# Two attention steps back to back in a fused attention and MLP kernel, the second one in the MLP's activation banks

## The chip, the cores and the metric

The kernel runs on one core of a Trainium2 chip. The metric is the device time of one execution in microseconds; the kernel before takes 1001.8 us (median of three runs, 1000.68 to 1001.87). The core has five engines that run side by side: TensorE (PE in the profile) for matmuls, VectorE (DVE), ScalarE (ACT), GpSimd (POOL), and SyncE (SP), which issues the transfers here. Matmul results go to PSUM, a small memory of eight banks, 512 float32 columns by 128 partitions each.

## The reference

A kernelised (random feature) attention feeds an MLP with layer normalisation and a residual. Batch 8, 8 heads, sequence 576, head dimension 64, 128 features; the model width is 512 and the hidden width 2048, and the sequence rows of all batches together are 4608.

```python
def phi(x):
    proj = np.einsum('bhsd,md->bhsm', x, omega)
    sq = np.sum(x * x, axis=-1, keepdims=True) / 2.0
    h = proj - sq
    h = h - np.max(h, axis=-1, keepdims=True)
    return np.exp(h) / np.sqrt(m)
q_p, k_p = (phi(q_s), phi(k_s))
kv = np.einsum('bhsm,bhsd->bhmd', k_p, v)
z = np.sum(k_p, axis=2)
num = np.einsum('bhsm,bhmd->bhsd', q_p, kv)
den = np.einsum('bhsm,bhm->bhs', q_p, z)[..., None] + 1e-06
attn = num / den
...
xn = (x - mu) / np.sqrt(var + 1e-06) * g_ln
ch = np.maximum(xn @ w_ch1, 0.0) @ w_ch2
return x + ch
```

## The kernel before

**Attention.** The work is cut into blocks of 128 rows. Four kinds of step put attention matmuls on TensorE, and each writes a pair of neighbouring PSUM banks:

- A *key step* (`gen_k`, matmuls L502) projects a block of keys for all eight heads: 16 matmuls that contract over 64 rows (64*128 in the profile: the upper or the lower half of the rows of the array, the "row" shape). VectorE then takes the maxima over both banks (L505), ScalarE does eight exponentials (L511), four for each bank, and each bank is given back after its four. The result is the tile kp, of which there are two. Each batch has four whole blocks; the remainders of two batches share a fifth.
- A *sums step* (`gen_sums`, L537) multiplies the features of one or two key blocks by the values: 32 matmuls per block that fill 64 columns of the array (128*64, the "col" shape). From batch 1 on the first four blocks are taken in twos and the remainder alone. The sum is copied or added to the tile kv; the kp tiles come free with the last matmul.
- A *query step* (`gen_q`) projects a block of queries: in the first eight blocks with 4 matmuls in the row shape (L580), and later with 4 matmuls in the whole array's shape (L598 and L599, 128*128). The features then go through a copy (L250 or L252), a maximum over the partitions on GpSimd (L610), a subtraction (L615) and an exponential (L618).
- An *output step* (`gen_x`, L657) multiplies a block's query features by kv: 32 matmuls in the col shape. VectorE divides by the denominator (L664 to L668) and takes the row statistics (L685, L687).

**MLP.** Nine tiles of 512 rows. Each tile's four blocks are normalised and transposed on TensorE (`gen_xnT1`, L740) into one tile xnT. Then 16 hidden slices `f` follow: `mm1(t, f)`, 12 matmuls of 128x512 into one bank of hidden activations (L767 to L769), `relu` (L778 on ScalarE, L780 on VectorE), and `mm2(t, f)`, 12 matmuls into the four accumulator banks (L800 to L802). Each product takes three matmuls, since both factors are split into a high and a low part. `gen_mlp` issues them in the order `mm1(f)`, `mm2(f-1)`, `mm1(f+1)`, `mm2(f)`; at a tile's end `mm2(15)` comes ahead of the next tile's `mm1(0)`. `result` (L815) adds the residual and writes the tile out.

**PSUM.** While the MLP runs, banks 0 and 1 (`b_at`) serve the attention steps and the transposes, banks 2 and 3 (`b_h`) the hidden activations and the transposes, and banks 4 to 7 the accumulators:

```python
    b_at, b_h, b_acc = banks[0:2], banks[2:4], banks[4:8]
```

An attention step therefore waits for the pair `b_at`, one step at a time.

**Order.** The order of the instructions on each engine is planned ahead, when the program is built, by the class `Plan`. Each piece of work is a generator (`Part`) with a rank; it yields what it wants next: a `"run"` on an engine with a cost in us, a `"wait"` for something made, a `"get"` of a buffer or a `"pair"` of banks. `Plan.run` takes the part that can start first, and among those that can start then the one with the lowest key (the rank, lowered by 100 while it holds banks). The MLP has the highest rank of the working parts (`LAST`, 10000), so that an attention step goes ahead of the MLP's next three matmuls as soon as it is ready and the pair is free; a part counts as ready for TensorE 0.45 us (`SLACK`) after its inputs are planned to be there. The plan charges an attention step in the row or col shape with 0.37 us (`VISIT`) beyond its matmuls. The ranks of the attention are places in the MLP: a hidden slice counts 2 and a tile `NS` = 32. A key block `c` of batch `b` has the rank `NS * (b * S // T) - 30 + 2 * c`, the sums of a group one more than its last key block, query block `i` of tile `t` has `NS * t - 22 + 2 * i`, and its output step has 6 more.

Buffers bound how far the attention runs ahead: two kp tiles, three tiles of values, three kv tiles, five quad tiles for query features, and nine tiles x, of which the current MLP tile holds four for its residual.

Of the kernel before, what the change touches and what calls it, by code (L numbers as in the profile page):

```python
# [41 lines left out]
class Part:  # L42


    def __init__(self, rank, order, gen, after):
        self.rank, self.order = rank, order
        self.holds = 0
        self.gen = gen
        self.after = after
        self.eng, self.end = None, 0.0  # L50
        self.lat = 0.0
        self.want = None

    @property
    def key(self):

        return (self.rank - (Plan.HOLDER if self.holds else 0), self.order)

    def seen(self):

# [7 lines left out]
class Plan:  # L68
# [13 lines left out]
    LOCK = 1.0  # L82
    FILL, IDLE = 10000, 20000
    HOLDER = 100
    BIAS = {PE: 0.0, ACT: 0.2, DVE: 0.5, POOL: -0.2, SP: 0.0}
    DMA_LATENCY = 2.0

    def __init__(self):
        self.free_at = dict.fromkeys((PE, ACT, DVE, POOL, SP), 0.0)
        self.dma_at = 0.0  # L90
        self.ready = []
        self.blocked = []
        self.made = {}
        self.places = {}
        self.cur = None
        self.count = 0

    def add(self, rank, gen):
        self.count += 1
# [19 lines left out]
    def meet(self, part):  # L119

        kind, what = part.want[:2]
        if kind == "wait" and what in self.made:
            part.after = max(part.after, self.made[what])
            return True
        if kind == "get":
            count = part.want[2] if len(part.want) > 2 else 1
            free = sorted((n for n in what if n in self.places), key=self.places.get)[:count]
            if len(free) == count:
                for name in free:
                    part.after = max(part.after, self.places.pop(name))  # L130
                    part.holds += name[0] == "b" and part.rank < Plan.FILL
                return free if len(part.want) > 2 else free[0]
        if kind == "pair":
            free = [p for p in what if all(n in self.places for n in p)]
            if free:
                pair = min(free, key=lambda p: max(self.places[n] for n in p))
                for name in pair:
                    part.after = max(part.after, self.places.pop(name))
                    part.holds += part.rank < Plan.FILL
                return pair  # L140
        (self.blocked if kind in ("wait", "get", "pair") else self.ready).append(part)
        return None

    def wake(self, wanted):
        for part in sorted((p for p in self.blocked if wanted(p.want)), key=lambda p: p.key):
# [5 lines left out]
    def free(self, *names):  # L151
        for n in names:
            assert n not in self.places, n
            self.places[n] = self.cur.seen()
            self.cur.holds -= n[0] == "b" and 0 < self.cur.holds
            self.wake(lambda w: (w[0] == "get" and n in w[1]) or (w[0] == "pair" and any(n in p for p in w[1])))

    def done(self, key):
# [11 lines left out]
        return min(times, key=lambda t: t[0] + t[2] + queue[t[1]])  # L170

    def run(self):
        while self.ready:
            queue = dict(Plan.BIAS)
            for p in self.ready:
                if len(p.want[1]) == 1:
                    ((e, cost),) = p.want[1].items()
                    if p.ready(e) <= self.free_at[e]:
                        queue[e] += cost
            now = {part: self.starts(part, queue) for part in self.ready}  # L180
            start, eng, _ = min(t for p, t in now.items() if p.rank != Plan.IDLE)
            for p in [p for p in self.ready if p.rank == Plan.IDLE]:
                t, e, cost = now.pop(p)
                if t <= start and all(t + cost <= o[0] for o in now.values() if o[1] == e):
                    now = {p: (t, e, cost)}
                    start, eng = t, e
                    break
            mine = [p for p in now if now[p][1] == eng]
            part = min((p for p in mine if now[p][0] <= start), key=lambda p: p.key)
            start, _, cost = now[part]  # L190
            self.ready.remove(part)
            part.eng = eng
            part.lat = part.want[2] if len(part.want) > 2 and part.want[2] != "two" else Plan.LAT[eng]
            if eng == SP:
                self.free_at[SP] = start + 0.65
                part.end = self.dma_at = max(self.dma_at, start + Plan.DMA_LATENCY) + cost
                part.end += 1.0
            else:
                self.free_at[eng] = part.end = start + cost
            self.advance(part, eng)  # L200
        assert not self.blocked, [(p.key, p.gen.__name__, p.want) for p in self.blocked]


@with_exitstack
def favor_ffn(ctx, tc, kT, kTr, vF, vR, qT, qD, omT, gT, w1, w2, out):
# [18 lines left out]
    plan = Plan()  # L224
# [70 lines left out]
    mlp_on = []  # L295
# [3 lines left out]
    def at_now():  # L299
        return b_at if mlp_on else banks  # L300

    def visit():
        return VISIT if mlp_on else 0.1

    def pairs_now():
        return (b_at,) if mlp_on else tuple(banks[i : i + 2] for i in range(0, 8, 2))
# [163 lines left out]
    def gen_k(b, c, kraw, early, owners, t_v, n_kp, last):  # L470
# [22 lines left out]
            done(("v", b, c))  # L493

        plan.add(rank, values())
        t_b = yield "pair", pairs_now()
        yield "run", {PE: visit() + 0.95}, 0.03
        pk = two(t_b).rearrange("p s (a b) -> p s a b", b=M)
        for p in range(NP):
            for h in range(2):  # L500
# [17 lines left out]
    def gen_sums(o, group, g, last):  # L518
        for key in group:
            yield wait("v", *key)  # L520
            yield wait("kp", *key)
        if g:
            yield wait("kvmm", o, g - 1)
        else:
            t_kv = yield "get", n_kv
            kvs[o] = t_kv, heads_of(t_kv)
        if o:
            t_b = yield "pair", pairs_now()
        else:
            t_b = pvs[0] = banks[6:8]  # L530
        yield "run", {PE: visit() + 0.94 * len(group)}, 0.03
        pv = two(t_b, 4 * (D + 1)).rearrange("p s (a b) -> p s a b", b=D + 1)
        for h in range(H):
            for i, key in enumerate(group):
                kp, v = kps[key][1], kps[key][2][o][1]
                for a in (0, D):
                    nc.tensor.matmul(  # L537
                        pv[a : a + D, h // 4, h % 4], kp[:, slot(h), a : a + D], v[:, h],
                        start=i == 0 and (o > 0 or g + h % 4 == 0),
                        stop=i == len(group) - 1 and (o > 0 or (last and h % 4 == 3)),  # L540
                    )
        for key in group:
            free(kps[key][2][o][0])
            kps[key][3] -= 1
            if not kps[key][3]:
                free(kps[key][0])
        done(("kvmm", o, g))
        if o == 0 and not last:
            return
        out = kvs[o][1].rearrange("p (s a) b -> p s (a b)", s=2)  # L550
        pv = two(t_b, 4 * (D + 1))
        if o and g:
            yield wait("kv", o, g - 1)
            yield dve(8 * (D + 1))
            nc.vector.tensor_tensor(out=out, in0=pv, in1=out, op=ALU.add)
        else:
            eng = yield "run", {ACT: 0.53, DVE: 0.61}
            copy(eng, out, pv)
        free(*t_b)
        done(("kv", o, g))  # L560
        if last:
            done(("kvall", o))


    def gen_q(c):
# [3 lines left out]
        if c < QF:  # L569
# [2 lines left out]
            nc.sync.dma_start(qraw, qT[c].rearrange("p a b -> p (a b)"))  # L572
            yield wait("om")
            free(*q_turn)
            t_b = yield "pair", pairs_now()
            yield "run", {PE: visit() + 0.92}, 0.03
            pq = two(t_b)
            for h in range(2):
                a = slice(h * D, (h + 1) * D)
# [2 lines left out]
        else:  # L582
# [8 lines left out]
            yield dve2(8 * P)  # L591
            nc.vector.tensor_tensor(out=qs[D:P], in0=qraw[D:P], in1=f32(qs[D:P]), op=ALU.subtract)
            free(t_q, *q_turn)
            t_b = yield "pair", pairs_now()
            yield us(PE, 0.92)
            pq = two(t_b)
            for h in range(2):
                nc.tensor.matmul(pq[:, h], om_hi, qs[:, h], start=True, stop=False)  # L598
# [42 lines left out]
    def gen_x(c, b_turn):  # L641
# [7 lines left out]
        x = tile_of(t_x, [P, DM])  # L649
        dn = tile_of(t_d, [P, H]).rearrange("p (s a) -> p s a", s=2)  # L650
        t_p, phi = phis[c]
        t_b = yield "pair", pairs_now()
        yield "run", {PE: visit() + 0.94}, 0.03
        pn = two(t_b, 4 * (D + 1)).rearrange("p s (a b) -> p s a b", b=D + 1)
        for h in range(H):
            for a, b in parts:
# [96 lines left out]
    def mm1(t, f):  # L753
# [7 lines left out]
        t_b = yield "get", b_h  # L761
        ph = bank(t_b)
        for k in range(NK):
            yield us(PE, 3 * 0.227)
            w = wparts[1, f if f < NK else f // NK * NK + k]
            cs = slice((k if f < NK else f % NK) * P, ((k if f < NK else f % NK) + 1) * P)
# [22 lines left out]
    def mm2(t, f):  # L789
# [4 lines left out]
        for i in range(TC):  # L794
            if f == 0:
                t_b = yield "get", (b_acc[i],)
                accs[i] = bank(t_b)
            yield us(PE, 3 * 0.227)
            cs = slice(i * P, (i + 1) * P)
            nc.tensor.matmul(accs[i], hl[:, 0, cs], w[:, 0], start=(f == 0), stop=False)  # L800
# [31 lines left out]
            plan.cur.after = plan.cur.end + (0.0 if cold else WARM)  # L832

    def gen_mlp():
        last = None
        for t in range(NT):
            for f in range(NF):
                if f == 0 and last:
                    yield from mm2(*last)
                    last = None  # L840
                yield from mm1(t, f)
                if last:
                    yield from mm2(*last)
                last = t, f
        yield from mm2(*last)
# [26 lines left out]
LINE = 16  # L872
FIRST = 6
N_BIG, N_QUAD = 4, 5
VISIT = 0.37
QF = 2 * TC
EARLY, BEFORE = 1, ("x", 3)
GATE_K, GATE_Q = 3, 3
# [45 lines left out]
```

## Time and profile before

| What | us |
|---|---|
| median of three runs | 1001.8 |
| the profiled execution | 1001.66 |
| its span | 999.9 |
| TensorE busy | 991.8 |
| VectorE busy | 448.8 |
| ScalarE busy | 343.7 |
| GpSimd busy | 121.3 |
| first MLP matmul starts | 42.43 |
| last MLP matmul starts | 995.69 |

The span is the time from the first to the last record of the profiled execution; its own time also holds what lies around the span. In a row of the groups stand line, engine, operation, output and input with their shapes, the count, the busy time, the mean of one in ns, and the idle time of the engine ahead of them. In a row of the timeline stand the start, the duration, the engine and the line; rows of one line that follow each other are merged, with their count. Records of matmuls overlap: 128x512 matmuls that follow each other have records of 0.39 us.

### The profile page before, as it was taken

The page shows a single profiled execution, that of the slowest core. Times are in us where ns is not written, and L with a number is a line of the kernel's source. Part 1 is how long each engine was busy: PE and PEld are TensorE (multiplying, and loading weights), DVE is VectorE, ACT ScalarE, POOL GpSimd, SP SyncE. Part 2 cuts the span into 40 slices and gives each one's busy share as a digit, 9 for nine tenths or more (in the row PEclk, how much of TensorE's full clock was granted, in tenths as well). Part 3 has the DMA queues.
Part 4 walks back from the last instruction along what each step waited for, and adds up shares of the span by engine and source line. Part 5 has one row for each costly group of instructions (what it writes and reads, how often), then busy time and mean ns, then how long its engine had stood idle before and what let it go on. Part 6 is the DMA issues. An engine that isn't in the chain of part 4 may idle for free.

```text
span 999.9 us, 16072 instructions
## 1 busy us (share of the span) xinstructions
PE 991.8 (99%) x6888; PEld 804.7 (80%) x6888; DVE 448.8 (45%) x749; ACT 343.7 (34%) x698; POOL 121.3 (12%) x44
## 2 busy tenths in 40 slices
PE   9999999999999999999999999999999999999998
PEld 7778778788878888878887888888888888888886
DVE  6999965553374432743167213731472142113112
ACT  7778644343443432343025312320242121111110
POOL 5010211212202200130003100410041000000000
PEclk9999999999999999999999999999999999999999
DMA  9346323121132210311022001200210010001001
GB/s 352 149 157 234 128 85 117 55 74 54 54 103 89 71 58 0 117 55 54 1 86 73 12 1 64 65 0 1 75 53 1 1 43 1 1 1 43 1 0 43
DMA packets 26279, 64.18 MB, mean 64 GB/s; under 512 B 3040, under 2 KB 3168, under 8 KB 26208
## 3 DMA queue, kind: packets, MB, share of 16 engines
q1 hardware_dynamic: 26208, 63.16, 18.3%
q8 instruction: 54, 0.88, 0.4%
q14 instruction: 17, 0.14, 0.0%
HBM read 53.71 MB, written 9.44 MB: 63 GB/s over the span
## 4 chain that ended last, share of the span: by engine, by line
PE 90%; DVE 5%; ACT 2%; DMA 2%; POOL 1%; issue 1%; SPq 0%; POOLq 0%; ACTq 0%; DVEq 0%
PE b L800 13%; PE b L767 13%; PE b L802 12%; PE b L801 12%; PE b L769 12%; PE b L768 12%; PE b L657 4%; PE b L502 3%; PE b L537 3%; PE b L740 1%; PE b L598 1%; PE b L599 1%; POOL quad L610 1%; DVE w L382 1%; DMA w<-w 1%
## 5 line engine op out<-in xcount | busy, mean ns | idle before, releaser
L780 DVE SCALAR_TENSOR_TENSOR hid<-b,hid 128x512 fp32r<-128x512 f32 x144 | 99.4, 690 | 403.0 <-ACT hid L778 402.8
L800 PE MATMUL b<-w,hid 128*128 128x512 f32 x576 | 230.3, 400 | 0.0
L778 ACT ACTIVATE hid<-b 128x512 fp32r<-128x512 f32 x144 | 86.2, 599 | 419.2 <-PE b L769 419.2
L767 PE MATMUL b<-xnT,w 128*128 128x512 f32 x576 | 229.6, 399 | 0.0
L768 PE MATMUL b<-xnT,w 128*128 128x512 f32 x576 | 224.6, 390 | 0.0
L801 PE MATMUL b<-w,hid 128*128 128x512 f32 x576 | 224.5, 390 | 0.0
L802 PE MATMUL b<-w,hid 128*128 128x512 f32 x576 | 224.5, 390 | 0.0
L769 PE MATMUL b<-xnT,w 128*128 128x512 f32 x576 | 224.5, 390 | 0.0
L610 POOL PARTITION_ALL_REDUCE quad<-quad x34 | 112.9, 3333 | 634.9 <-ACT quad L250 439.9
L767 PEld LDWEIGHTS b<-xnT,w 128*128 128x128 f32 x576 | 108.0, 188 | 27.3 <-issue 2.3
L800 PEld LDWEIGHTS b<-w,hid 128*128 128x128 f32 x576 | 108.1, 188 | 24.7 <-issue 0.8
L802 PEld LDWEIGHTS b<-w,hid 128*128 128x128 f32 x576 | 108.1, 188 | 23.1
L769 PEld LDWEIGHTS b<-xnT,w 128*128 128x128 f32 x576 | 108.1, 188 | 23.1
L768 PEld LDWEIGHTS b<-xnT,w 128*128 128x128 f32 x576 | 108.2, 188 | 21.3 <-DVE w L416 0.3
L801 PEld LDWEIGHTS b<-w,hid 128*128 128x128 f32 x576 | 108.2, 188 | 20.7
L511 ACT ACTIVATE kp<-b,mb 128x128 f32<-128x128 f32 x264 | 74.3, 387 | 63.6 <-DVE mb L505 49.2
L505 DVE TENSOR_REDUCE mb<-b 128x8 f32<-128x1024 f32 x36 | 43.9, 1220 | 38.9 <-PE b L502 38.5
L618 ACT ACTIVATE quad<-quad 128x1024 f32<-128x1024 f32 x35 | 37.5, 1071 | 66.5 <-DVE quad L615 51.4
L615 DVE TENSOR_TENSOR quad<-quad,quad 128x1024 f32<-128x1024 f32 x34 | 47.4, 1394 | 18.2 <-POOL quad L610 18.0
L250 ACT COPY quad<-b 128x1024 f32<-128x1024 f32 x33 | 33.4, 1013 | 52.2 <-PE b L599 42.8
L657 PEld LDWEIGHTS b<-kv,quad 128*64 128x64 f32 x1120 | 35.3, 137 | 12.1 <-issue 4.8
L657 PE MATMUL b<-kv,quad 128*64 128x65 f32 x1120 | 39.9, 224 | 0.5 <-DVE quad L252 0.5
(84 smaller groups left out, 727.8 us busy)
## 6 DMA issues: line engine op xcount, KB each, us to landing
w<-w SPq DMA_DIRECT2D x32, 512.0 KB, 6.8
quad<-qD SPq DMA_DIRECT2D x28, 512.0 KB, 3.4
out<-x SPq DMA_DIRECT2D x36, 256.0 KB, 2.0
v<-vF SPq DMA_DIRECT2D x28, 260.0 KB, 3.0
wide<-kT SPq DMA_DIRECT2D x28, 256.0 KB, 3.1
wide<-qT SPq DMA_DIRECT2D x7, 256.0 KB, 4.5
v<-vR SPq DMA_DIRECT2D x6, 260.0 KB, 2.8
w<-vF SPq DMA_DIRECT2D x4, 260.0 KB, 4.8
```

The lines of the kernel that those rows point to most:

```text
L511: nc.scalar.activation(out=kp[:, j], in_=pk[:, s, j % 4], func=AF.Exp, scale=1.0, bias=mb[:, j : j + 1])
L610: nc.gpsimd.partition_all_reduce(mx.rearrange("p a b -> p (a b)"), qc.rearrange("p a b -> p (a b)"), P, bass_isa.ReduceOp.max)
L615: nc.vector.tensor_tensor(out=qc, in0=qc, in1=mx, op=ALU.subtract)
L657: nc.tensor.matmul(pn[a : a + D, h // 4, h % 4], phi[:, h % 2, h // 2, a : a + D], kvs[b][1][:, h], start=True, stop=True,)
L767: nc.tensor.matmul(ph, w[:, 0, cs], xnT[:, 0, k], start=(k == 0), stop=False)
L768: nc.tensor.matmul(ph, w[:, 1, cs], xnT[:, 0, k], start=False, stop=False)
L769: nc.tensor.matmul(ph, w[:, 0, cs], xnT[:, 1, k], start=False, stop=(k == NK - 1))
L778: nc.scalar.activation(out=hl[:, 0], in_=ph, func=AF.Relu)
L780: nc.vector.scalar_tensor_tensor(out=hl[:, 1], in0=ph, scalar=0.0, in1=f32(hl[:, 0]), op0=ALU.max, op1=ALU.subtract)
L800: nc.tensor.matmul(accs[i], hl[:, 0, cs], w[:, 0], start=(f == 0), stop=False)
L801: nc.tensor.matmul(accs[i], hl[:, 0, cs], w[:, 1], start=False, stop=False)
L802: nc.tensor.matmul(accs[i], hl[:, 1, cs], w[:, 0], start=False, stop=(f == NF - 1))
```

## The change

The plan gets a further kind of request, `"visit"`, by which an attention step asks for TensorE while the MLP runs. It names a mode (`"row"`, `"col"`, or `"all"` for the whole array's shape) and a cost. Visits wait in a list of their own, and the MLP's generators call `plan.serve` to place them.

- Ahead of every three matmuls of `mm1` and `mm2`, `serve(False)` may place one waiting step, if both banks of `b_at` are free: one in mode `"all"` if fewer than two row or col steps wait, and a row or col step if its rank is below the MLP's place (`plan.at`) or it has waited over 50 us (`PATIENCE`).
- Ahead of a `mm1`, if the MLP has issued a `mm1` and a `mm2` since the last lend, `serve(True)` may do more: if two steps of the same mode wait and the banks of `b_at` and of `b_h` are all free, it places both back to back, the later one by key first and in `b_h` (the loan). The plan charges the switch of 0.37 us once. Then `mm2` of the slice before is issued ahead of this `mm1`, and the `mm1` waits for a bank of `b_h` as always. The evacuation of the lent banks gets a key lowered by 1500.
- If the MLP itself is blocked in the plan and the pair is free, the waiting step that is ready first is placed.

Ahead of the MLP's first matmul the steps ask for a pair as before. No matmul, evacuation or transfer is added or removed.

The core of the diff; left out are new fields and the same replacement of `"pair"` by `visit` in the other steps.

```diff
@@ class Part
     def key(self):
 
-        return (self.rank - (Plan.HOLDER if self.holds else 0), self.order)
+        return (self.rank - (Plan.HOLDER if self.holds else 0) - (Plan.LENT if self.lent else 0), self.order)
@@ class Plan
+    LENT = 1500
+    SWITCH = 0.37
+    PATIENCE = 50.0
...
+    def go(self, part, pair, cost):
+        self.take(part, pair)
+        start = max(part.ready(PE), self.free_at[PE])
+        part.eng, part.lat = PE, 0.03
+        self.free_at[PE] = part.end = start + cost
+        grant, part.grant = part.grant, None
+        self.advance(part, grant)
+
+    def open(self, pair):
+        return all(n in self.places and self.places[n] + Plan.SLACK <= self.free_at[PE] for n in pair)
+
+    def serve(self, lend):
+
+        now = self.free_at[PE]
+        waiting = sorted((p for p in self.visits if p.ready(PE) <= now), key=lambda p: p.key)
+        if not waiting or not self.open(self.pair):
+            return False
+        narrow = [p for p in waiting if p.want[1] != "all"]
+        if lend and len(narrow) > 1 and self.open(self.loan):
+            pairs = [(a, b) for i, a in enumerate(narrow) for b in narrow[i + 1 :] if a.want[1] == b.want[1]]
+            if pairs:
+                a, b = pairs[0]
+                self.go(b, self.loan, Plan.SWITCH + b.want[2])
+                self.go(a, self.pair, a.want[2])
+                return True
+        for p in waiting:
+            if p.want[1] == "all":
+                if len(narrow) < 2:
+                    self.go(p, self.pair, p.want[2])
+                    return False
+            elif p.rank < self.at or now - p.ready(PE) > Plan.PATIENCE:
+                self.go(p, self.pair, Plan.SWITCH + p.want[2])
+                return False
+        return False
...
     def run(self):
-        while self.ready:
+        while self.ready or self.visits:
+            if self.visits and self.mlp in self.blocked and all(n in self.places for n in self.pair):
+                part = min(self.visits, key=lambda p: (p.ready(PE), p.key))
+                cost = part.want[2] + (Plan.SWITCH if part.want[1] != "all" else 0.0)
+                self.take(part, self.pair)
+                part.want = "run", {PE: cost}, 0.03
+                self.ready.append(part)
...
-    def visit():
-        return VISIT if mlp_on else 0.1
+    plan.pair, plan.loan = b_at, b_h
+
+    def visit(mode, cost):
+        if mlp_on:
+            return (yield "visit", mode, cost)
+        t_b = yield "pair", pairs_now()
+        yield "run", {PE: cost + (0.0 if mode == "all" else 0.1)}, 0.03
+        return t_b
@@ gen_k
-        t_b = yield "pair", pairs_now()
-        yield "run", {PE: visit() + 0.95}, 0.03
+        t_b = yield from visit("row", 0.95)
...
@@ mm1 (and mm2 likewise)
         for k in range(NK):
+            plan.serve(False)
             yield us(PE, 3 * 0.227)
...
@@ gen_mlp
-        last = None
+        last, rested = None, False
+        plan.mlp = plan.cur
         for t in range(NT):
             for f in range(NF):
-                if f == 0 and last:
-                    yield from mm2(*last)
-                    last = None
+                plan.at = NS * t + 2 * f
+                if last:
+                    lent = False
+                    if rested:
+                        yield us(PE, 0.0)
+                        lent = plan.serve(True)
+                    if lent or f == 0:
+                        yield from mm2(*last)
+                        last = None
                 yield from mm1(t, f)
+                rested = last is not None
                 if last:
                     yield from mm2(*last)
                 last = t, f
```

More of the change, by code (lines that the diff above doesn't have):

```diff
@@ L52, in __init__ @@
         self.want = None
+        self.grant = None
+        self.lent = 0
     @property
     def key(self):
-        return (self.rank - (Plan.HOLDER if self.holds else 0), self.order)
+        return (self.rank - (Plan.HOLDER if self.holds else 0) - (Plan.LENT if self.lent else 0), self.order)
     def seen(self):
@@ L96, in __init__ @@
         self.count = 0
+        self.visits = []
+        self.mlp = None
+        self.pair, self.loan, self.at = (), (), 0
     def add(self, rank, gen):
@@ L140, in meet, with take @@
                 return pair
-        (self.blocked if kind in ("wait", "get", "pair") else self.ready).append(part)
-        return None
+        if kind == "visit":
+            self.visits.append(part)
+        else:
+            (self.blocked if kind in ("wait", "get", "pair") else self.ready).append(part)
+        return None
+    def take(self, part, pair):
+        for name in pair:
+            part.after = max(part.after, self.places.pop(name))
+        part.holds += len(pair)
+        part.lent = len(pair) if pair == self.loan else 0
+        self.visits.remove(part)
+        part.grant = pair
+    def go(self, part, pair, cost):
[29 more added lines that the diff above has]
+        return False
     def wake(self, wanted):
@@ L155, in free @@
             self.cur.holds -= n[0] == "b" and 0 < self.cur.holds
+            self.cur.lent -= n[0] == "b" and 0 < self.cur.lent
             self.wake(lambda w: (w[0] == "get" and n in w[1]) or (w[0] == "pair" and any(n in p for p in w[1])))
@@ L199, in run @@
                 self.free_at[eng] = part.end = start + cost
-            self.advance(part, eng)
-        assert not self.blocked, [(p.key, p.gen.__name__, p.want) for p in self.blocked]
+            grant, part.grant = part.grant, None
+            self.advance(part, grant or eng)
+        assert not self.blocked and not self.visits, [(p.key, p.gen.__name__, p.want) for p in self.blocked]
 @with_exitstack
@@ L527, in gen_sums @@
         if o:
-            t_b = yield "pair", pairs_now()
+            t_b = yield from visit("col", 0.94 * len(group))
         else:
             t_b = pvs[0] = banks[6:8]
-        yield "run", {PE: visit() + 0.94 * len(group)}, 0.03
+            yield "run", {PE: 0.1 + 0.94 * len(group)}, 0.03
         pv = two(t_b, 4 * (D + 1)).rearrange("p s (a b) -> p s a b", b=D + 1)
@@ L574, in gen_q @@
             free(*q_turn)
-            t_b = yield "pair", pairs_now()
-            yield "run", {PE: visit() + 0.92}, 0.03
+            t_b = yield from visit("row", 0.92)
             pq = two(t_b)
@@ L593, in gen_q @@
             free(t_q, *q_turn)
-            t_b = yield "pair", pairs_now()
-            yield us(PE, 0.92)
+            t_b = yield from visit("all", 0.92)
             pq = two(t_b)
@@ L651, in gen_x @@
         t_p, phi = phis[c]
-        t_b = yield "pair", pairs_now()
-        yield "run", {PE: visit() + 0.94}, 0.03
+        t_b = yield from visit("col", 0.94)
         pn = two(t_b, 4 * (D + 1)).rearrange("p s (a b) -> p s a b", b=D + 1)
@@ L797, in mm2 @@
                 accs[i] = bank(t_b)
+            plan.serve(False)
             yield us(PE, 3 * 0.227)
@@ L874 @@
 N_BIG, N_QUAD = 4, 5
-VISIT = 0.37
 QF = 2 * TC
```

## The prediction

> **What bounds the kernel now.** I read the page's busy shares and its forty slices first, to see whether one engine sets the time throughout.
>
> ```profile
> span 999.9 us, 16072 instructions
> PE 991.8 (99%) x6888; PEld 804.7 (80%) x6888; DVE 448.8 (45%) x749; ACT 343.7 (34%) x698; POOL 121.3 (12%) x44
> PE   9999999999999999999999999999999999999998
> DVE  6999965553374432743167213731472142113112
> PEclk9999999999999999999999999999999999999999
> ```
>
> TensorE is busy in every slice at full clock; VectorE is full only in the first tenth. A busy TensorE need not be an efficient one, since matmul records overlap, so next come the groups of matmuls from the first MLP matmul on, the busy time of that stretch, and the first and last MLP matmul.
>
> ```profile
> L800 PE MATMUL b<-w,hid 128*128 128x512 f32 x576 | 230.3, 400 | 0.0
> ...
> L769 PE MATMUL b<-xnT,w 128*128 128x512 f32 x576 | 224.5, 390 | 0.0
> L657 PE MATMUL b<-kv,quad 128*64 128x65 f32 x1024 | 36.9, 224 | 0.5 <-DVE quad L252 0.5
> L502 PE MATMUL b<-om,wide 64*128 64x128 f32 x496 | 36.5, 285 | 0.9 <-ACT quad L250 0.6 <-DVE x L668 0.4
> L537 PE MATMUL b<-v,kp 128*64 128x65 f32 x1088 | 36.1, 223 | 0.0
> ...
> L580 PE MATMUL b<-wide,om 64*128 64x512 f32 x16 | 4.5, 641 | 0.0
> ```
>
> ```profile
> 42.43:1000.00 957.57, 952.24 (x6323) 773.00 (x6320) 417.23 (x687) 314.06 (x628) 106.50 (x32) 1.00 0.16 54
> ```
>
> ```profile
> 42.43 0.47 PE L767 MATMUL b<-xnT,w 128*128 128x512 f32 x1
> ...
> 995.69 0.39 PE L802 MATMUL b<-w,hid 128*128 128x512 f32 x1
> ```
>
> From 42.43 us on the idle column of these groups sums to 1.4 us: TensorE hardly waits for anybody. A change can gain here only by taking TensorE time away. The counts give the steps placed among the MLP's matmuls: key steps 496/16 = 31 and early query steps 16/4 = 4 (both 64*128, the "row" shape), sums steps 1088/32 = 34 sets of 32 (14 steps with two sets and 6 with one, by the code's groups), output steps 1024/32 = 32 (the "col" shape, 128*64). That is 35 row and 52 col steps, 87 in all. The later query steps use the MLP's own 128*128 shape.
>
> Next, what one of them costs. The timeline of TensorE, around a sums step with one set, one with two sets, and around a key step with its evacuation by VectorE and ScalarE (start, duration, engine, line):
>
> ```profile
> 317.64 0.39 PE L769 MATMUL b<-xnT,w 128*128 128x512 f32 x1
> 317.96 1.15 PE L537 MATMUL b<-v,kp 128*64 128x65 f32 x32
> ...
> 319.61 0.39 PE L802 MATMUL b<-w,hid 128*128 128x512 f32 x1
> ```
>
> ```profile
> 343.97 0.39 PE L800 MATMUL b<-w,hid 128*128 128x512 f32 x1
> ...
> 345.11 0.39 PE L802 MATMUL b<-w,hid 128*128 128x512 f32 x1
> 345.43 2.09 PE L537 MATMUL b<-v,kp 128*64 128x65 f32 x64
> ...
> 348.01 0.39 PE L769 MATMUL b<-xnT,w 128*128 128x512 f32 x1
> ```
>
> ```profile
> 348.70 0.40 PE L769 MATMUL b<-xnT,w 128*128 128x512 f32 x1
> 349.03 1.16 PE L502 MATMUL b<-om,wide 64*128 64x128 f32 x16
> ...
> 350.24 1.22 DVE L505 TENSOR_REDUCE mb<-b 128x8 f32<-128x1024 f32 x1 [1.89 <-PE b L502]
> ...
> 350.70 0.39 PE L769 MATMUL b<-xnT,w 128*128 128x512 f32 x1
> ...
> 351.56 1.14 ACT L511 ACTIVATE kp<-b,mb 128x128 f32<-128x128 f32 x4 [6.07 <-DVE v L492]
> ...
> 353.05 1.17 ACT L511 ACTIVATE kp<-b,mb 128x128 f32<-128x128 f32 x4
> ...
> 355.11 1.16 PE L502 MATMUL b<-om,wide 64*128 64x128 f32 x16
> ```
>
> From 343.97 to 345.11 lie five matmuls: 0.228 us each. From the last MLP matmul before a step to the third after it, three such intervals (0.68) are the MLP's own; the rest is the step. One set: 319.61 - 317.64 - 0.68 = 1.29. Two sets: 348.01 - 345.11 - 0.68 = 2.22. A second set directly behind a first costs 2.22 - 1.29 = 0.93, so the entry and exit of a col step cost 1.29 - 0.93 = **0.36 us**. This is what the change shares between two steps. A key step costs 350.70 - 348.70 - 0.68 = 1.32.
>
> **The change part by part.** *Pairs, the gain.* A col step directly behind another saves 0.36. No key step follows another inside the MLP in this trace; the nearest rows are in the prologue, where a key step is followed at once by a query step of the same 64*128 shape:
>
> ```profile
> 14.52 1.16 PE L502 MATMUL b<-om,w 64*128 64x128 f32 x16
> 15.52 1.03 PE L580 MATMUL b<-wide,om 64*128 64x512 f32 x4
> ```
>
> The key step occupies 15.52 - 14.52 = 1.00 there, against 1.32 in the MLP: 0.32 saved. The upper bound is the col saving, 0.36; the lower one zero, if two key steps should get in each other's way, which nothing here suggests. I take 0.33, nearest the prologue rows.
>
> [...]
>
> *How many pairs.* At most 87/2 = 43, or 15 us. The code decides how many form. A pair needs two ready steps of one shape at a point ahead of a first-layer group, with both bank pairs open, and not directly after another lend, so at most 8 times per MLP tile. Other steps go alone as soon as their rank is below the MLP's place. In the first tile, and until about a third of the second, attention runs behind its ranks: there the four early query steps, the four key steps and two sums of batch 1, the first four output steps and some six more (about 20) go alone on becoming ready; I give them one pair. About 67 steps remain: 27 key steps, 40 col. For key steps the buffers set the pattern: there are two kp tiles, freed by the sums step of the two, so keys come in twos, but after a batch's fifth block one partner is missing: eight of nine at best. I take 9 pairs. For col steps: four output steps per tile come ready together when the result of the tile before gives back its x tiles, so two pairs per tile for tiles 2 to 6, about 9 or 10; a two-set sums step comes ready alone and needs a waiting output step, or goes by itself when due: I count a third of them, 4 or 5. Sum 9 + 14 + 1 = **24 pairs**: 15 x 0.36 + 9 x 0.33 = 8.4 us. Bounds of the count: 8 (2.8 us) if nearly all go as due, 38 (13 us) if nearly every step finds its partner.
>
> *The loan.* The lent banks must be back when the first-layer group behind the second-layer group wants one: after two steps (2 x 0.93) and twelve matmuls (12 x 0.228), 4.6 us after the loan's first matmul. A key step's first bank is free when its first four exponentials end: 351.56 + 1.14 - 349.03 = 3.7 us; the second bank, 353.05 + 1.17 - 349.03 = 5.2, is wanted only by the next group, at 7.3. So the cover is 0.9 us. An output step's banks come back sooner:
>
> ```profile
> 406.65 1.15 PE L657 MATMUL b<-kv,quad 128*64 128x65 f32 x32
> ...
> 408.29 0.69 DVE L668 TENSOR_TENSOR x<-b,dn 128x512 f32<-128x512 f32 x1
> ```
>
> 2.3 us. So the loan costs nothing where VectorE and ScalarE take it promptly, and there the parts behind a lent step are put ahead of others in the plan. Where an operation is already running ahead of it, the cover can go. In this trace it did:
>
> ```profile
> 152.22 1.16 PE L502 MATMUL b<-om,wide 64*128 64x128 f32 x16
> ...
> 155.89 1.14 ACT L511 ACTIVATE kp<-b,mb 128x128 f32<-128x128 f32 x4 [0.43 <-DVE mb L505]
> ```
>
> 155.89 + 1.14 - 152.22 = 4.8 us, so 0.2 too late, and TensorE would stand with the first-layer group and everything behind it. I charge 0.5 us for all loans.
>
> *Waiting.* Steps now wait for a partner, up to 50 us or their rank. No engine waits meanwhile, since the second half of the time has VectorE at a few tenths; what moves is only when evacuations and the next loads (same number and size, on SP's queue) happen. The query steps that need no switch are held while two switching steps wait; their products are due a quarter tile or more before the next tile wants them. I charge 0.5 us for one late tile start, the most likely at the end of the first tile, where output steps come last. The added zero-cost order point issues no instruction, and an early first-layer group is only reordered against a second-layer group.
>
> **Sum** against the profiled execution: span 999.9 - 8.4 + 0.5 + 0.5 = 992.5. That execution took 1001.66 us, 1.8 outside the span, and stands 0.1 under the median of the three runs, 1001.8. The forecast is 1001.8 - 7.4 = **994.4 us**, a gain of 0.7%.
>
> **The rivals.** *Few pairs.* The key step above keeps the attention pair closed from 349.03 until the next at 355.11, 6 us, about one MLP place of 24 x 0.228 = 5.5 us: the order point often finds it closed, steps fall due, and go alone. For it: this spacing. Against: in the later tiles there are places without any step. With 5 to 14 pairs, say 10, it gives 1001.8 - 3.5 + 0.5 = 998.8.
>
> *Nearly all pair.* With 36 pairs 1001.8 - 12.5 = 989.3. For it: the trace leaves TensorE no other waits, and the waiting steps lose nothing by waiting. Against: the odd key blocks and the early tile.
>
> *Slower: the loan comes back late.* The place is the first-layer group behind each lent key step. A VectorE operation of 1.22 and a ScalarE one of 1.14 running ahead would make the first bank 2.4 us later than 3.7, so 1.5 later than wanted. It decides from the point where lateness over all 24 pairs averages what a pair saves, 0.35; ten key pairs late by 1.1 each give 11 - 8.4, so 1001.8 + 2.6 = 1004.4. Against: after the first tenth VectorE is mostly free.
>
> *It does not do what it says.* If the open-banks condition is nearly never met at the order point, all steps go alone as before, near 1001.5.
>
> **How the numbers follow.** Forecast (15 to 35 pairs) 0.55; few pairs 0.18; nearly all 0.11; late loans 0.10; no effect 0.06. The likeliest case's own range is 990 to 997.5. For 8 in 10 it goes down to 988.5, which takes in most of the full pairing, and up to 1001.0, which takes in the few pairs; what is left out is the late loan, no effect and the very best count. About 0.2%, 2 us, is what a measurement of this kernel can tell from no change: faster is the forecast, nearly all, and four fifths of the few pairs, 0.81; within 0.2% the rest of few pairs and most of no effect, 0.09; slower 0.10.
>
> **What would show it.** In the changed trace: the same counts per line, but records of L502 or L657 with twice their matmuls, or L537 directly beside L657, ahead of a second-layer matmul; these joined records number about 24. From the last MLP matmul ahead of a joined col pair to the third behind it, 1.29 + 0.93 + 0.68 = 2.90 us. The idle column of the first layer's L767 stays near zero if the loans come back in time; waits there for ScalarE's L511 mean the late loan. A gap ahead of the first L767 of a tile, with transposes close before it, means held steps. I am wrong if the joined records are under 15 or over 35, or if the span differs from the joined count times 0.35 by more than 3 us.

## The result, and the profile after

The changed kernel takes **988.9 us** (median; 988.33 to 989.26) against 1001.55 of the kernel before beside it: a ratio of 0.9874, 95% interval 0.9857 to 0.9892. It is 12.7 us faster, and 5.5 us faster than forecast.

The page's head and slices after:

```profile
span 987.1 us, 16033 instructions
PE 979.3 (99%) x6888; PEld 804.4 (81%) x6888; DVE 450.0 (46%) x739; ACT 351.8 (36%) x708; POOL 120.7 (12%) x44
PE   9999999999999999999999999999999999999998
DVE  6999966436523435264334433316535152123112
PEclk9999999999999999999999999999999999999999
```

TensorE bounds the kernel as before, with the same 6,888 matmuls, and its busy time is 991.8 - 979.3 = 12.5 us shorter. So the time was taken out of TensorE's own work, and not out of waits. The groups of matmuls from the first MLP matmul on, and the last MLP matmul:

```profile
L604 PE MATMUL b<-v,kp 128*64 128x65 f32 x1088 | 35.4, 223 | 0.0
L721 PE MATMUL b<-kv,quad 128*64 128x65 f32 x1024 | 34.9, 223 | 1.2 <-DVE hid L845 1.2
L569 PE MATMUL b<-om,wide 64*128 64x128 f32 x496 | 32.8, 280 | 0.0
```

```profile
42.06 0.47 PE L832 MATMUL b<-xnT,w 128*128 128x512 f32 x1
...
982.99 0.39 PE L868 MATMUL b<-w,hid 128*128 128x512 f32 x1
```

The counts of the key steps (L569, formerly L502), the sums steps (L604, formerly L537) and the output steps (L721, formerly L657) are the same. From the first to the last MLP matmul it is 940.9 us, where it was 953.3: 12.3 us of the gain lie there.

The timeline of TensorE around a key pair and around a pair of output steps:

```profile
166.28 0.39 PE L868 MATMUL b<-w,hid 128*128 128x512 f32 x1
166.60 2.06 PE L569 MATMUL b<-om,wide 64*128 64x128 f32 x32
...
169.15 0.40 PE L868 MATMUL b<-w,hid 128*128 128x512 f32 x1
```

```profile
414.81 0.39 PE L868 MATMUL b<-w,hid 128*128 128x512 f32 x1
415.13 2.09 PE L721 MATMUL b<-kv,quad 128*64 128x65 f32 x64
...
417.72 0.39 PE L868 MATMUL b<-w,hid 128*128 128x512 f32 x1
```

Read as the prediction read a single step (first row to third matmul behind, less three intervals of 0.227), a key pair costs 169.15 - 166.28 - 0.68 = 2.19 us, where two single steps cost 2 x 1.30 = 2.60: **0.41 saved**. (1.30 is the usual cost of a single key step in the kernel before; the one that the prediction read, 1.32, is among the dearest of those that wait for nothing.) An output pair costs 2.23 in these rows, and 2.22 in most of the nine, where two cost 2 x 1.29 = 2.58: **0.36 saved**. Over the whole timeline there are 30 such pairs: 12 of key steps, 9 of two output steps, 7 of an output and a sums step, 2 of two sums steps. 12 x 0.41 + 18 x 0.36 = 11.4 us. The expectations below were written with 0.42 and 11.5, from a single key step taken as 1.31. What TensorE waited within the MLP stage, read as what a step costs above its kind's usual value, hardly changed: 2.1 us before (four places), 2.0 after. The MLP also began 0.4 us earlier, which is not the change's: in a second run of the changed kernel it began at 42.43, as in the kernel before, and in the runs below that start lies anywhere from 41.4 to 42.6. This accounts for all but 0.8 us of the 12.7.

### The profile page after: what moved, and what is told of

It reads as the page before. It is cut to its first block, busy times and chain, and to the rows that moved or that the text cites. A ratio compares the mean times of both kernels' runs of the same rounds, so it can differ in the third digit from the quotient of the medians.

```text
span 987.1 us, 16033 instructions
## 1 busy us (share of the span) xinstructions
PE 979.3 (99%) x6888; PEld 804.4 (81%) x6888; DVE 450.0 (46%) x739; ACT 351.8 (36%) x708; POOL 120.7 (12%) x44
## 4 chain that ended last, share of the span: by engine, by line
PE 94%; DMA 2%; ACT 1%; DVE 1%; issue 1%; POOL 1%; SPq 0%; POOLq 0%
PE b L866 14%; PE b L832 13%; PE b L833 13%; PE b L867 13%; PE b L868 13%; PE b L834 13%; PE b L721 4%; PE b L604 3%; PE b L569 3%; PE b L804 2%; PE b L664 1%; PE b L663 1%; PE b L407 1%; DMA w<-w 1%; POOL quad L675 1%
## 5 line engine op out<-in xcount | busy, mean ns | idle before, releaser
L832 PE MATMUL b<-xnT,w 128*128 128x512 f32 x576 | 226.5, 393 | 0.0
L843 ACT ACTIVATE hid<-b 128x512 fp32r<-128x512 f32 x144 | 86.0, 597 | 378.5 <-PE b L834 373.9
L832 PEld LDWEIGHTS b<-xnT,w 128*128 128x128 f32 x576 | 108.1, 188 | 24.2 <-issue 0.8
L578 ACT ACTIVATE kp<-b,mb 128x128 f32<-128x128 f32 x264 | 72.4, 393 | 58.5 <-DVE mb L572 58.4
L680 DVE TENSOR_TENSOR quad<-quad,quad 128x1024 f32<-128x1024 f32 x34 | 59.0, 1736 | 19.4 <-POOL quad L675 19.0
L658 DVE TENSOR_TENSOR quad<-quad,quad 64x1024 fp32r<-64x1024 f32 x28 | 40.8, 1477 | 28.7 <-ACT quad L656 28.5
L721 PEld LDWEIGHTS b<-kv,quad 128*64 128x64 f32 x1120 | 34.6, 137 | 9.3 <-issue 6.2
```

The lines of the kernel that those rows point to most:

```text
L578: nc.scalar.activation(out=kp[:, j], in_=pk[:, s, j % 4], func=AF.Exp, scale=1.0, bias=mb[:, j : j + 1])
L680: nc.vector.tensor_tensor(out=qc, in0=qc, in1=mx, op=ALU.subtract)
L721: nc.tensor.matmul(pn[a : a + D, h // 4, h % 4], phi[:, h % 2, h // 2, a : a + D], kvs[b][1][:, h], start=True, stop=True,)
L832: nc.tensor.matmul(ph, w[:, 0, cs], xnT[:, 0, k], start=(k == 0), stop=False)
L843: nc.scalar.activation(out=hl[:, 0], in_=ph, func=AF.Relu)
```

## The experiments

### A change of shape between the two steps

Theory: the gain is the entry and exit that two adjacent steps of one shape share. Rival: it comes from the new order. To split adjacency from order, one small matmul in the MLP's full shape is put into each pair, without telling the plan, so that all else stays in place: between the steps, or, as the control, ahead of the first.

```diff
+                self.mark = "first"
                 self.go(b, self.loan, Plan.SWITCH + b.want[2])
+                self.mark = "second"
                 self.go(a, self.pair, a.want[2])
+                self.mark = None
@@ visit
-            return (yield "visit", mode, cost)
+            t_b = yield "visit", mode, cost
+            if plan.mark == "second":   # the control: "first"
+                nc.tensor.matmul(bank(t_b[0], 64), spin[:, 0:P], spin[:, 0:64], start=True, stop=True, skip_group_check=True)
+            return t_b
```

> The changed kernel's order with one small full-shape matmul (128 rows by 128 columns, 64 columns moved) put between the two steps of each of its 30 pairs; everything else is as in the changed kernel. Theory (the gain is the entry and exit that two adjacent steps of one shape share): the gain is lost, 12 key pairs x 0.42 + 18 col pairs x 0.36 = 11.5 us, and 30 small matmuls come on top: 1000.5 to 1004 us. Rival (the gain comes from the new order and the new waiting times, not from adjacency): only the 30 small matmuls, 989 to 992 us.

> The control: the same 30 small full-shape matmuls, each ahead of the first step of a pair, where TensorE is still in the MLP's full shape. Both theories: 989 to 992 us, which prices the small matmul itself (0.03 to 0.1 us each).

Measured: between the steps 997.97 us, ahead of them 990.63. The control prices the small matmul at (990.63 - 988.9)/30 = 0.06 us. Between the steps it costs 7.3 us more, 0.24 a pair. The rival falls: with the same order and the same waits (2.0 us), most of the gain is gone once the shape changes in between. But the 11.5 expected didn't all go: the time lies between the two ranges, and the timeline shows why. The key pair with the small matmul between:

```profile
135.55 0.39 PE L875 MATMUL b<-w,hid 128*128 128x512 f32 x1
135.87 1.16 PE L576 MATMUL b<-om,wide 64*128 64x128 f32 x16
136.97 0.20 PE L374 MATMUL b<-spin 128*128 128x64 bf16 x1
137.10 1.16 PE L576 MATMUL b<-om,wide 64*128 64x128 f32 x16
138.19 0.50 PE L873 MATMUL b<-w,hid 128*128 128x512 f32 x1
...
138.75 0.40 PE L875 MATMUL b<-w,hid 128*128 128x512 f32 x1
```

138.75 - 135.55 - 0.68 = 2.52, against 2.19 for the pair and 2.60 for two single steps. So the two changes of shape are 0.3 of the 0.41, the small matmul included. The last 0.1 belongs to coming back to the MLP: from the first to the third MLP matmul behind the step it is 138.75 - 138.19 = 0.56 us, where two intervals take 0.45. Two single steps pay this 0.1 twice, a pair once, with or without the small matmul inside it. Adjacency saves both.

### Two steps of different shape

Only a row and a col step may pair:

```diff
-            pairs = [... if a.want[1] == b.want[1]]
+            pairs = [... if a.want[1] != b.want[1]]
...
-                self.go(a, self.pair, a.want[2])
+                self.go(a, self.pair, a.want[2] + (0.0 if a.want[1] == b.want[1] else 0.2))
```

> Only two steps of different shape (one row, one col) may pair; the plan charges 0.2 us between them. Its order holds 19 pairs. Theory (what is shared is a change of shape at each seam, four for two single steps, two for a pair of one shape, three for a mixed pair): a mixed pair costs 2.62 to 2.40 instead of 1.31 + 1.29 = 2.60, by the prologue's seams (key to sums 1.09, sums to key 1.08 against 0.89 to 0.93 bare) about 0.2 saved each: joined records of some 2.4, and 1001 - 3.8 = 997 us, more if steps arrive late. Rival (adjacency alone counts, whatever the shape): 19 x 0.38 = 7.2, joined records of 2.2, 994 us.

Measured: 998.41 us, ratio 0.9974 (0.9963 to 0.9984). A mixed pair:

```profile
134.40 0.39 PE L868 MATMUL b<-w,hid 128*128 128x512 f32 x1
134.72 1.16 PE L569 MATMUL b<-om,wide 64*128 64x128 f32 x16
135.81 1.15 PE L721 MATMUL b<-kv,quad 128*64 128x65 f32 x32
136.89 0.50 PE L866 MATMUL b<-w,hid 128*128 128x512 f32 x1
...
137.47 0.40 PE L868 MATMUL b<-w,hid 128*128 128x512 f32 x1
```

137.47 - 134.40 - 0.68 = 2.39, where the two alone cost 1.30 + 1.29 = 2.59: 0.20 saved, half of what a pair of one shape saves. Each change of shape is paid, and the theory's 2.40 holds. The 19 pairs would save 3.8 us; the time fell by 2.6 only. One key step in that run costs 1.6 more than usual, a wait.

### Fewer pairs

```diff
-    PATIENCE = 50.0
+    PATIENCE = 0.0     # the other run: 10.0
```

> PATIENCE = 0: a waiting step goes alone at the first place that is open, so its order holds 2 pairs instead of 30, with the new request, the order points and the lend still there. Theory: 1001.6 - 2 x 0.36 = about 1000.9, or 1000.5 if the earlier MLP start of the changed kernel (0.4 us) stays. Rival (new order alone): clearly under 998.

> PATIENCE = 10: a step goes alone after 10 us without a partner; its order holds 14 pairs (6 key pairs, 8 col pairs). Theory (the time is the number of pairs times the price in the trace, 0.42 a key pair and 0.36 a col pair, plus a few waits): 6 x 0.42 + 8 x 0.36 = 5.4 us under the kernel before, 995.6, or against the run with 2 pairs (998.9) 4.7 less, 994.2. Rival (the first few pairs bring most of it, or the waiting itself does): under 991 or over 998.

```diff
-            pairs = [... if a.want[1] == b.want[1]]
+            pairs = [... if a.want[1] == b.want[1] == "row"]
```

> Only row steps may pair; col steps wait for their rank or 50 us and go alone. Its order holds 12 key pairs. Theory with the changed kernel's own price of a key pair (0.42): 1001.6 - 5.1 - 0.4 = 996.1 us. With the prologue's price that the prediction took (0.33): 997.2 us. Rival (held steps arrive late at tile starts once they find no partner): 998 or more, with waits of TensorE ahead of the first matmuls of tiles.

| Kernel | pairs: key, col | us | at 0.41 and 0.36 saved | us plus saved |
|---|---|---|---|---|
| before | 0, 0 | 1001.0 | 0 | 1001.0 |
| PATIENCE 0 | 0, 2 | 998.9 | 0.7 | 999.6 |
| row only | 12, 0 | 997.0 | 4.9 | 1001.9 |
| PATIENCE 10 | 6, 8 | 995.2 | 5.3 | 1000.5 |
| changed | 12, 18 | 988.9 | 11.4 | 1000.3 |

The rows come from three sets of runs, in which the kernel before took 1001.0 to 1001.6. The last column would be one number if pairs were all. It varies by 2.3 us, and the pairs' share by 11.4: the pairs carry the gain, in proportion to their number. The rest are waits and the start of the MLP, which each order has its own. With PATIENCE 0 the time came out 1.6 to 2 us lower than I expected from the pairs: of the four places where TensorE waited in the kernel before (2.1 us), one (0.7 us) is left, and the MLP started 0.6 us earlier. The row-only run came out at 997.0, near the 997.2 of the lower price for a key pair, but not for that reason: each of its twelve key pairs costs 2.19 us in its timeline, as in the changed kernel, and its waits come to 3.2 us, 2.0 of them at five output steps.

### What holding steps back costs without partners

```diff
-            pairs = [... if a.want[1] == b.want[1]]
+            pairs = [... if a.want[1] == b.want[1] == "col"]
```

> Only col steps may pair; key steps and early query steps wait for their rank or 50 us and go alone, and the query steps of the full shape are still held while two row or col steps wait. Its order holds 13 col pairs. Theory (holding back costs nothing only as long as partners are found; without them the output steps come late and the MLP waits at tile starts): the pairs save 4.7 us but waits of several us per tile come in: over 1005 us, with gaps of TensorE ahead of the first matmuls of tiles. Rival (holding back is free, as the prediction's 0.5 us said): 1001 - 4.7 = 996 to 997 us.

Measured: 1021.68 us, ratio 1.0204 (1.0189 to 1.0219): slower than the kernel before, by 20.6 us. TensorE at the start of the third MLP tile, then busy time and granted clock there (of TensorE, its weight loads, VectorE, ScalarE and GpSimd, each with its count; the last three columns are the clock, the transfers' share and GB/s):

```profile
249.47 1.16 PE L569 MATMUL b<-om,wide 64*128 64x128 f32 x16
...
261.57 0.39 PE L868 MATMUL b<-w,hid 128*128 128x512 f32 x1
261.89 1.16 PE L569 MATMUL b<-om,wide 64*128 64x128 f32 x16
265.62 0.50 PE L663 MATMUL b<-quad,om_hi 128*128 128x512 f32 x1 [2.57 <-DVE quad L680]
265.96 0.40 PE L664 MATMUL b<-quad,om_lo 128*128 128x512 f32 x1
...
270.10 0.80 PE L663 MATMUL b<-quad,om_hi 128*128 128x512 f32 x1 [1.10 <-ACT quad L312]
270.69 0.63 PE L664 MATMUL b<-quad,om_lo 128*128 128x512 f32 x1
...
273.28 2.00 PE L721 MATMUL b<-kv,quad 128*64 128x65 f32 x32 [1.10 <-ACT quad L312]
...
277.41 3.50 PE L604 MATMUL b<-v,kp 128*64 128x65 f32 x64 [2.13 <-DVE x L732]
...
282.80 0.49 PE L832 MATMUL b<-xnT,w 128*128 128x512 f32 x1
...
284.05 0.40 PE L832 MATMUL b<-xnT,w 128*128 128x512 f32 x1
```

```profile
262.00:283.00 21.00, 12.46 (x157) 9.64 (x158) 11.14 (x16) 9.80 (x18) 8.78 (x3) 0.67 0.26 91
267.70:280.00 12.30, 7.89 (x86) 6.07 (x88) 5.98 (x8) 4.59 (x6) 6.43 (x2) 0.50 0.18 65
```

The tile's query steps, output steps and transposes come here one after the other, each waiting for the evacuation of the one before, with no MLP work beside them. Read to the fourth MLP matmul behind, this place takes 284.05 - 261.57 - 4 x 0.227 = 21.6 us for steps that cost 8.4 elsewhere; another at 602 us takes 17.5 for 7.1. Together that is 23.6 us too much, against 4.7 saved by 13 pairs, and so most of the 20.6. What came late here is a query step, held by the rule that no query step goes while two row or col steps wait. By the order that this kernel's plan makes, these two are key steps, which may not pair in this run: both wait from 212 us on, the tile's last query step is ready at 222, the first key step goes alone after 50 us (249.47 above), the query step at 258.85, and its output step and transposes are still to come when the MLP wants the tile. At 602 us it is the same. So holding back is not free: a held step that finds no partner also holds others. In the changed kernel two waiting key steps pair, and its timeline has no such gap.

### When the loan comes back

```diff
-                self.go(b, self.loan, Plan.SWITCH + b.want[2])
-                self.go(a, self.pair, a.want[2])
+                self.go(a, self.pair, Plan.SWITCH + a.want[2])
+                self.go(b, self.loan, b.want[2])
```

> The lent banks go to the second step of a pair instead of the first, so they come back one step (0.9 us) later; 31 pairs, 12 of them key pairs. Theory (a lent key step has about 0.9 us of cover, and as second step its maxima also queue behind the first step's): the first bank comes back some 4.8 us after the pair's first matmul, where the first-layer group wants it after 4.6: TensorE waits 0.2 to 0.5 us behind each key pair, seen ahead of L832's counterpart: 991 to 995 us. Rival (there is more cover than that): no waits behind key pairs, 988 to 989.5 us.

In the changed kernel the lent banks go to the step that is issued first; here to the one behind it. Measured: 989.77 us, ratio 0.9885 (0.9871 to 0.9900), 0.9 over the changed kernel with one pair more, and between the two ranges. The waits of weight loads in this run, and the timeline of a key pair:

```profile
PEld b L832 <- ACT kp L578: 2.5, 12, 0.2
...
PEld b L604 <- DVE xnT L810: 2.2, 2, 1.9
```

```profile
168.07 2.06 PE L569 MATMUL b<-om,wide 64*128 64x128 f32 x32
...
170.54 4.33 ACT L578 ACTIVATE kp<-b,mb 128x128 f32<-128x128 f32 x16 [4.48 <-DVE mb L572]
172.91 0.45 PE L832 MATMUL b<-xnT,w 128*128 128x512 f32 x1
```

Twelve waits, one for each key pair, by ScalarE's exponentials, as the theory has it, but of the weight load and only 0.2 us: the first-layer group started 172.91 - 168.07 = 4.84 us behind the pair's first matmul, against 4.6 in my working, and it is 4.84 in the changed kernel too, so nearly all the lateness went into the exit that the working left out. The matmuls themselves lost under 0.1 us a pair. A single wait of 1.9 us at a sums step (at 155 us) is the larger loss. In the changed kernel the wait row for L832 by L578 isn't there: the loan comes back in time for all twelve.

### Later due times

```diff
-            elif p.rank < self.at or now - p.ready(PE) > Plan.PATIENCE:
+            elif p.rank < self.at - 4 or now - p.ready(PE) > Plan.PATIENCE:
...
-    PATIENCE = 50.0
+    PATIENCE = 45.0
```

> A candidate: steps fall due four ranks (two hidden slices) later and PATIENCE is 45; its order holds 32 pairs instead of 30, 12 of them key pairs. Theory: two more col pairs, 0.7 us less than the changed kernel if no wait comes in: 988.2 us. Rival (the later steps bring waits): 989 or more.

> The changed kernel unchanged, beside the candidate with later due times on the same chip: 988.9 us.

> The candidate of the last set (due four ranks later, PATIENCE 45, 32 pairs) against the changed kernel on one chip. Theory: two more col pairs, 0.7 us, and no new waits: 0.6 to 1.1 us below the changed kernel. Rival: the difference of the last set was between chips, within 0.3 us of the changed kernel.

First set: 987.85 us, ratio 0.9865 (0.9851 to 0.9880). On one chip with the changed kernel: 987.78 (987.57 to 988.1) against 989.06 (988.7 to 989.55), ratios to before 0.9869 (0.9855 to 0.9884) and 0.9882 (0.9865 to 0.9898). The single times don't overlap and the medians differ by 1.3 us, in the same direction as in the first set; the two intervals against the kernel before do overlap. Two more col pairs are 0.7 us of it. In the two traces of this set the stretch from the first to the last MLP matmul is 1.0 us shorter (940.0 against 940.9), and the MLP begins 0.7 us earlier, which I don't count as the order's. It is the fastest kernel here, by about 0.1%.

## Why the prediction was right, and where its sizes were off

**What bounds, and what the change takes.** Right: TensorE is full in both traces, and the gain is TensorE time at the seams. The 0.36 us that the prediction drew from the sums steps with one and two sets is what a col pair saves. The small matmul between the steps (0.24 us a pair more than ahead of them) shows that it is adjacency in one shape; the mixed pair (0.20 saved, against 0.36 to 0.41) shows that each change of shape costs.

**The price of a key pair** was mis-sized: taken as 0.33 from a prologue where a key step is followed by an early query step, measured 0.41 in every one of the twelve pairs. It also lies above the 0.36 that the prediction gave as the upper bound. In the prologue the second step was of another kind, and its start is no measure for a second key step: in the pair the second key step adds 2.19 - 1.30 = 0.89, not 1.00. This is 12 x 0.08 = 1.0 us.

**The count** was mis-sized most: 24 against 30. The 9 key pairs were an allowance under the ceiling by buffers that the prediction named, eight of nine; the plan reaches the ceiling, 12. Of col pairs it has 18 rather than 14: 9 of output steps, as counted, but 7 sums steps found a waiting output step where I counted 4 or 5, and the sums of the two halves of a shared key block, ready together, pair twice, which I had left out. At the prediction's own prices six more pairs are about 2.1 us.

**Loans and waiting**, charged 0.5 us each, cost nothing net: 2.0 us of waits against 2.1. But not for the reason given, and with some luck: the loan cost more than its charge, 1.3 us at two pairs, and the other waits happened to fall from 2.1 to 0.7 in the new order. With PATIENCE 0, where only two pairs form, they fell as well, so pairing isn't what removed them. The lent key step's banks came back in time at every pair (the first-layer group behind it shows no delay in any of the twelve). The loan's wait is at its other end, in taking the banks. Twice a pair of output steps stood 0.6 us for the hidden bank of the slice before (rows of several engines, in order of time):

```profile
431.67 3.29 POOL L675 PARTITION_ALL_REDUCE quad<-quad  x1
432.03 2.68 DVE L680 TENSOR_TENSOR quad<-quad,quad 128x1024 f32<-128x1024 f32 x1
434.75 1.06 ACT L683 ACTIVATE quad<-quad 128x1024 f32<-128x1024 f32 x1 [2.15 <-DVE quad L680]
435.00 1.23 DVE L680 TENSOR_TENSOR quad<-quad,quad 128x1024 f32<-128x1024 f32 x1 [0.28 <-POOL quad L675]
435.71 0.58 ACT L843 ACTIVATE hid<-b 128x512 fp32r<-128x512 f32 x1
436.32 0.69 DVE L845 SCALAR_TENSOR_TENSOR hid<-b,hid 128x512 fp32r<-128x512 f32 x1
437.07 2.09 PE L721 MATMUL b<-kv,quad 128*64 128x65 f32 x64 [0.59 <-DVE hid L845]
```

VectorE's subtraction took 2.68 us beside GpSimd's reduction, so the exponential behind it came late, the slice's `relu` (L843) stood behind that on ScalarE, and the bank that the pair needed came free only at 437.0. The prediction looked at who waits for the loan's return and not at what the loan waits for.

**Sum.** 994.4 was forecast. The count takes 2.1 us off it, the price of key pairs 1.0, the charge for waits 1.0: 990.3. The rest, 1.4 us, are the earlier start of the MLP (0.4), the slightly lower median of the kernel before in this comparison (0.2) and the 0.8 that the rows don't assign. All of these point the same way, so the time fell outside the likeliest case's own range, 990 to 997.5, and only 0.4 us inside the wide one, 988.5 to 1001.0: the mechanism held, and that the wide range held was close.

**The rivals.** *Nearly all pair* gave 989.3 and is nearest to the time, with 30 pairs at a higher price in place of 36. *Few pairs* rested on the attention pair being closed at the order point; what it had against it decided: a step that isn't due simply waits for the next order point. It is what happens with PATIENCE 10 (14 pairs, 995.2). *The loan late* is real in mechanism and small: even lent to the second step, 0.2 us of weight load per key pair. *It does not do what it says* falls with the 30 pairs in the timeline. The danger lay elsewhere, in the held steps themselves: the prediction charged them 0.5 us, since the products are due late, and the col-only run shows 23.6 us at two tile starts where two key steps find no partner and keep a query step back.

## What to carry to other kernels

Where an engine that is never idle pays to enter and leave a mode, grouping the visits is worth their number times the seam (here 30 pairs, 11.4 of the 12.7 us), and the seam can be read beforehand from steps that come in single and double length; take it from the same kind of step, or keep both ends. A rule that holds work back until it finds a partner needs its release tested with the partners taken away (here 20.6 us over the kernel before). When buffers are lent, look at both ends: what waits for their return, and what must finish before they can be taken.

## What the runs showed of the hardware

A two-input VectorE subtraction on 128x1024 took 1.23 us alone and 2.68 beside GpSimd's reduction over partitions (rows above). Which of the two starts first matters: within the MLP stage of the two traces, the 13 subtractions that began inside a reduction (10 after, 3 before) took 2.68 to 2.95, and the four that were already running when one began took 1.22 to 1.23, while that reduction took 4.1 to 4.2 instead of 3.2 to 3.3. With pairs in the order the mean of that line rose, from 1394 ns (L615 before) to 1736 (L680 after).

Where TensorE waited at a tile start in the col-only run, the granted clock was 0.67 on average over 21 us and 0.50 from 267.7 to 280.0, and a 128x512 matmul's record rose from 0.40 to 0.63 us (L664 at 265.96 and 270.69). So this place lost more than its waits: its matmuls came slower too, 0.43 us from one start to the next (270.69 to 271.12), where it is 0.23 ahead of it (258.85 to 259.08). The longest single wait ahead of the drop was 2.57 us; what brought the clock down no run here shows.
